# Attention and a Fourier-mixing layer on one core: which of batch 2's three token tiles is worked on alone, and first

## The chip, the cores and the metric

The kernel runs on one core of one Trainium2 chip. The core has five engines with a queue each: TensorE (PE, with its weight loads as PEld), VectorE (DVE), ScalarE (ACT), GpSimd (POOL) and SyncE (SP, which only issues DMAs here). The metric is device time in microseconds; less is better.

## The reference, cut to what matters

```python
def _attn_ref(q, k, v, tau):             # q, k, v: (8, 12, 448, 64)
    q_n = q / (norm(q, axis=-1) + 1e-06)
    k_n = k / (norm(k, axis=-1) + 1e-06)
    scores = q_n @ k_n.T / tau
    attn = softmax(scores)
    return attn @ v

def _moe_ref(x, w_ch1, w_ch2):           # x: (8, 448, 768)
    mixed = real(fft(fft(x, axis=1), axis=2))
    u = x + mixed
    un = (u - mean(u)) / sqrt(var(u) + 1e-06)     # over the last axis
    ch = relu(un @ w_ch1) @ w_ch2                 # 768 -> 3072 -> 768
    return u + ch
```

The attention's output, heads side by side, is the `x` of the second part. There are 8 batches of 448 tokens.

## The kernel before, in words

**Stages of a batch.** For each batch b the kernel loads q, k and v, normalises q and k (squares on ACT, sums on DVE, scaling on POOL, from batch 2 on with DMA transposes into `QT` and `KT`), computes scores (PE, L1464 and L1477), exponentials (ACT, L1442) and the product with v (PE, L1495 and L1501; result `X`). `ORDER` is the order of the six head pairs. Then comes the Fourier transform as matmuls with sine and cosine tables: folding of `X` on DVE (`fold`), the first product over tokens (`fs0_b`, `fs1_b`: PE, L1632 and nearby), its copy out of PSUM (`te`), the second product over features (`fd0_b`, `fd1_b`: PE, L1682 and L1685), and on DVE and ACT the sums that give `U` (`qe`, `pq`, `u`; L1713, L1716, L1727). Each row block of `U` is a token tile: its mean, variance and scale (`ba`, `bs`, `ln2`, `rs`), the normalised tile (`un`, L1779), and a DMA transpose issued by SP (`tru`, L1800) into `UNT`, where PE reads it.

**Token tiles.** A batch gives the tiles A0 (rows 0 to 127 of the first half of the transform), A1 (the mirrored rows), Yt and, shared by an even batch and the odd one behind it, Zt. `A0` and `A1` come from the transform's first half (`fd0`), Yt from its second (`fd1`); one row of A1 is copied out of Yt (`u224`, L1747), so that A1 is only whole after that copy. An even batch has three tiles in the order A0, A1, Yt, an odd one four, 28 in all.

**Pairs and singles.** The feed-forward part takes tiles in the order of batches, two at a time, except those named in `ONES`, which are taken alone:

```python
ONES = ((0, 0), (2, 2))
...
        while x < len(order):
            n = 1 if order[x] in ONES else 2
            for y in range(n):
                b, i = order[x + y]
                self.slots[b][i] = 2 * (u % 2) + y
            self.pairs.append(order[x:x + n])
            u, x = u + 1, x + n
```

`(2, 2)` is tile 2 of batch 2, Yt. `slots` says which 128 columns of `UNT` a tile's transpose fills; the units take slots 0 and 1, then 2 and 3, in turn.

A unit's work on PE is a chain in fixed order (`self.main`): the hidden layer (`h..`, from `UNT` and `W1b`, L1864: 144 matmuls, of 256 columns for a pair, of 128 for a single), whose PSUM banks ACT and DVE empty with the ReLU into `HQ` (L1880), and the second layer (L2008, 384 columns). For a pair this is a product scheme with seven block products of 12 matmuls (`m1` to `m7`) in place of eight; it needs the sums and differences `s1` to `s4` over `HQ` on DVE (L2108, six instructions) and of the weights in `TX`. For a single it is four products of 12 (`y0` to `y3`) with one sum (`s5`). The results go to `OUTB` (`fa`, `fv`, `fm`, `fin`: ACT L2029, POOL L2034, DVE L2045); `store` writes A0 with a plain DMA from SP (L2059) and the others with an indirect DMA from POOL (L2067). Between the steps of a unit PE takes attention steps of the next batch and the transform's steps.

**What sets the order.** `build` lists all steps with their dependencies and a base priority (`op.prio`), then adds to each its entry of the table `SHIFT` (some 1,870 names; the key within an entry counts the steps of that name). `Plan.schedule` then fills the queue of each engine at build time: it takes, with costs from the tables `TIMES` and `FLOW`, the step that can start first, and among those that can start at the same time the one with the lowest priority. ACT and DVE may also wait a little for a step of much lower priority number. On the chip every engine's queue is in that fixed order, with semaphore waits. `HOME` fixes the engine of some steps of the start. `Plan.fill` puts dummy matmuls (L2258) where the plan leaves PE idle for long, mostly in the first 48 us.

Of the kernel before, what the change touches and what calls it, by code (L numbers as in the profile page):

```python
# [26 lines left out]
ONES = ((0, 0), (2, 2))  # L27
# [55 lines left out]
    "iota": {0: -4743.9411}, "iotak": {0: -3749.0012}, "cst": {0: 2295.738}, "iotad": {0: 1504.4864}, "rown": {0: 3564.9514},  # L83
    "tqd": {0: 5876.6502, 1: 5614.4443}, "trd": {0: 5875.7288}, "tpd": {0: -1558.5233, 1: 550.4848}, "tad": {0: 4737.392},
    "tqs": {0: 4545.6213, 1: 5636.9779}, "trs": {0: 4448.6198}, "tps": {0: -162.6304, 1: -1607.3824}, "tas": {0: -178.9521}, "ktd0": {0: 1975.3204},
# [4 lines left out]
    "mask": {0: 35657.0228}, "sinp": {0: 48649.0823}, "half": {0: 440.6683, 1: 3500.6271}, "sinn": {0: 17464.9799}, "ldt": {0: 44319.0778},  # L90
# [883 lines left out]
class Kern:  # L974
# [857 lines left out]
    def units(self):  # L1832
# [486 lines left out]
```

## Time and profile before

| what | value |
|---|---|
| median of three runs | 575.11 us (574.59 to 575.68) |
| the profiled execution's own time | 575.0 us |
| its span, first to last instruction | 573.2 us |
| granted TensorE clock, mean | 1.000 |
| busy: PE, PEld, DVE, ACT, POOL | 553.7, 432.9, 434.0, 392.9, 224.4 us |
| HBM traffic over the span | 110 GB/s |

How to read it: times are in microseconds from the start of the span, a matmul's mean in nanoseconds. PE's matmuls are pipelined, so one that takes 326 ns by its row does not hold the next one up for as long; the pace is read from how long a run of equal matmuls takes. The chain that ended last is followed back from the last instruction, so that each of its pieces is what the next one waited for or came behind. "issue" in it, and as what ended an idle time, is time for which the profile shows no releaser. A bracket behind a row of the timeline is the idle time of the engine ahead of it.

### The profile page before, as it was taken

Reading aid. Unit: us, or ns where it says so; the run is one execution under the profiler, and the core shown is the slowest. Engines: PE = TensorE matmul, PEld = TensorE weight load, DVE = VectorE, ACT = ScalarE, POOL = GpSimd, SP = SyncE. Lnnn points to the kernel's source line nnn. Section 1 sums busy time; section 2 is a strip of 40 time slices with the busy share of each in tenths; the row PEclk is TensorE's granted clock in tenths of the full one; section 3 lists DMA queues with packets and bytes.
Section 4 is the critical chain, followed back from the end, with each engine's and each line's share of the span. In section 5 each row is a group of like instructions: output and inputs, shape, how many; then the busy total and the mean of one; then the engine's idle time right before and its main releaser. Section 6 shows DMA issues by size and latency. Waiting matters only on the chain.

```text
span 573.2 us, 16025 instructions
## 1 busy us (share of the span) xinstructions
PE 553.7 (97%) x6616; PEld 432.9 (76%) x6616; DVE 434.0 (76%) x923; ACT 392.9 (69%) x734; POOL 224.4 (39%) x332
## 2 busy tenths in 40 slices
PE   3899999999999899999999999999999999999998
PEld 2578887686787687878778688687886876959695
DVE  9889868987469867986789669965679379886353
ACT  7998976576776885578648886686665761948171
POOL 8522414356328542702380736443524003041304
PEclk9999999999999999999999999999999999999999
DMA  9999997976359645963496569461691200132001
GB/s 213 170 241 202 164 195 108 163 173 111 111 82 113 158 88 111 155 145 70 95 157 76 99 138 125 105 140 23 136 87 27 72 2 17 42 48 66 24 34 56
DMA packets 183945, 62.19 MB, mean 108 GB/s; under 512 B 166688, under 2 KB 181664, under 8 KB 183872
## 3 DMA queue, kind: packets, MB, share of 16 engines
q1 hardware_dynamic: 129824, 38.35, 35.2%
q0 software_dynamic: 54048, 22.81, 32.1%
q8 instruction: 52, 0.85, 0.6%
q14 instruction: 21, 0.17, 0.1%
HBM read 51.90 MB, written 11.01 MB: 110 GB/s over the span
## 4 chain that ended last, share of the span: by engine, by line
PE 78%; DVE 8%; ACT 6%; issue 3%; POOL 2%; DMA 2%; SPq 1%; POOLq 0%; DVEq 0%; ACTq 0%
PE PS L1864 28%; PE PS L2008 26%; PE PS L1959 7%; PE PS L1501 5%; PE PS L1464 5%; PE PS L1495 2%; PE PS L1477 1%; DMA TX<-in_q_dram 1%; ACT F L1769 1%; POOL QH L1387 1%; DVE F L1547 1%; POOL OUTB L2034 1%; PE PS L1685 1%; DVE OUTB L2045 1%; DVE X L1521 1%
## 5 line engine op out<-in xcount | busy, mean ns | idle before, releaser
L1864 PE MATMUL PS<-UNT,W1b 128*128 128x256 bf16 (+1 forms) x1728 | 185.4, 264 | 0.3 <-DVE UNT L1797 0.2
L1442 ACT ACTIVATE E<-PS 128x900 bf16<-128x900 f32 (+1 forms) x192 | 148.7, 827 | 30.3 <-PE PS L1464 24.3
L1864 PEld LDWEIGHTS PS<-UNT,W1b 128*128 128x128 bf16 x1728 | 153.4, 98 | 20.1 <-issue 1.9
L2008 PE MATMUL PS<-W2b,HQ 128*128 128x384 bf16 x720 | 124.9, 326 | 0.0
L1387 POOL TENSOR_TENSOR QH<-STG,SM 128x256 bf16<-128x256 f32 x126 | 84.4, 696 | 86.8 <-DVE SM L1177 65.0
L2008 PEld LDWEIGHTS PS<-W2b,HQ 128*128 128x128 bf16 x720 | 68.8, 98 | 43.1 <-issue 0.4
L2034 POOL TENSOR_TENSOR OUTB<-OUTB,U 128x192 f32<-128x192 f32 x72 | 51.6, 737 | 118.2 <-ACT OUTB L2029 115.6
L2008 PE MATMUL PS<-TX,HQ 128*128 128x384 bf16 (+2 forms) x444 | 76.4, 322 | 0.9 <-DVE OUTB L2045 0.5
L1880 ACT ACTIVATE HQ<-PS 128x512 bf16<-128x512 f32 x86 | 51.2, 595 | 28.8 <-PE PS L1864 27.6
L2108 DVE TENSOR_TENSOR HQ<-HQ 128x1536 bf16<-128x1536 bf16 (+1 forms) x73 | 54.1, 744 | 12.2 <-ACT HQ L1880 7.0
L2008 PEld LDWEIGHTS PS<-TX,HQ 128*128 128x128 bf16 x444 | 41.5, 98 | 27.9 <-DVE OUTB L2045 2.4
L1374 ACT ACTIVATE QH<-STG 128x384 f32<-128x384 f32 x84 | 43.1, 519 | 17.6 <-DVE SM L1376 11.6
L1376 DVE TENSOR_REDUCE SM<-QH 128x6 f32<-128x384 f32 x84 | 45.3, 544 | 11.3 <-ACT QH L1374 11.0
L1501 PE MATMUL PS<-VB,E 128*128 128x65 bf16 x1152 | 51.6, 193 | 0.0
L2067 POOL DMA_INDIRECT out_dram<-OUTB,IDX x21 | 23.7, 1127 | 69.2 <-DVE OUTB L2045 43.4
L1501 PEld LDWEIGHTS PS<-VB,E 128*128 128x128 bf16 x1152 | 47.8, 97 | 1.3
L1880 DVE TENSOR_SCALAR HQ<-PS 128x512 bf16<-128x512 f32 x40 | 27.4, 685 | 23.9 <-PE PS L1864 23.8
L1495 PE MATMUL PS<-VZ,E 128*128 128x130 bf16 x192 | 41.6, 219 | 2.0 <-issue 1.9
L1727 DVE SCALAR_TENSOR_TENSOR U<-ACG,X 128x768 bf16<-128x768 f32 (+4 forms) x39 | 39.5, 1023 | 0.9
L2029 ACT ACTIVATE OUTB<-PS 128x384 f32<-128x384 f32 x36 | 17.7, 491 | 32.2 <-PE PS L2008 29.4
L1464 PE MATMUL PS<-QK 64*128 64x225 bf16 (+2 forms) x864 | 39.2, 227 | 0.5 <-ACT QK L1290 0.5
L1464 PEld LDWEIGHTS PS<-QK 64*128 64x128 bf16 x864 | 25.6, 95 | 13.2 <-issue 6.6
(195 smaller groups left out, 784.5 us busy)
## 6 DMA issues: line engine op xcount, KB each, us to landing
STG<-in_q_dram SPq DMA_DIRECT2D x18, 384.0 KB, 3.9
STG<-in_k_dram SPq DMA_DIRECT2D x18, 384.0 KB, 3.9
VB<-in_v_dram POOLq DMA_DIRECT2D x24, 192.0 KB, 6.4
W2b<-in_moe_w_ch_dram POOLq DMA_DIRECT2D x12, 384.0 KB, 7.4
W1b<-in_moe_w_ch_dram POOLq DMA_DIRECT2D x5, 768.0 KB, 14.7
out_dram<-OUTB SPq DMA_DIRECT2D x7, 384.0 KB, 2.7
W2b<-in_k_dram SPq DMA_DIRECT2D x2, 576.0 KB, 9.1
W2b<-in_q_dram SPq DMA_DIRECT2D x2, 576.0 KB, 15.9
```

The source lines that it names most:

```text
L1374: P.add("act", lambda a, sq=sq, src=buf[:, w * x:w * x + w]: a.activation(sq, src, ACTF.Square), t_act(w), pr, f"sq{i}_{b}", reads=bn, wri ...
L1376: P.add("dve", lambda v, o=SS[:, i, H // ns * x:H // ns * (x + 1)], sq=sq: v.tensor_reduce(o, sq.rearrange("p (h d) -> p h d", d=DH), AX.X ...
L1387: r = v.tensor_tensor(v3(qh)[:, h:h + 4], v3(buf)[:, h:h + 4], RN[:, i, h:h + 4].unsqueeze(2).to_broadcast((128, 4, DH)), AluOp.mult)
L1442: return a.activation(o, self.PS[:, bk:bk + nc_, 0:SQ2], ACTF.Exp, scale=1.0 / self.tau)
L1464: i = pe.matmul(self.PS[:, bk + h, c0:c0 + n], self.KT[r, jj, kt * 128:(kt + 1) * 128], self.QT[r, jj, cols], start=True, stop=True)
L1495: r = pe.matmul(o, st(6), self.VZ[:, j, :], start=not split, stop=(split and i == 0), skip_group_check=True)
L1501: r = pe.matmul(o[:, 65 * h:65 * h + 65], st(2 * kt + h), self.VB[:, kt, 2 * j + h, :], start=(split and i == h == kt == 0), stop=((not sp ...
L1864: r = pe.matmul(self.PS[:, bk, x * n:(x + 1) * n], self.W1b[:, j, ft * 128:(ft + 1) * 128], self.UNT[:, j, cs], start=(j == 0), stop=(j == ...
L1880: return e.activation(o, i, ACTF.Relu) if e is self.nc.scalar else e.tensor_relu(o, i)
L2008: r = pe.matmul(self.PS[:, bk, 0:n], lhs(f), rhs(f), start=(start and f == 0), stop=(stop and f == NF // 2 - 1), skip_group_check=True)
L2034: r = g.tensor_tensor(self.OUTB[:, ob, xs], self.OUTB[:, ob, xs], self.U[:, ut, xs], AluOp.add)
L2108: P.add("dve", lambda v: v.tensor_tensor(cs(o), cs(a), cs(bq), op), 0.16 + 0.3 * len(ks), -0.5, f"{nm}{ks[0]}_{b}", reads=rd, writes=[x fo ...
```

## The change

The constant `ONES` names tile 0 of batch 2 in place of tile 2. So batch 2's A0 becomes a unit of its own, worked on first, and A1 and Yt form the pair behind it. A0 keeps slot 0 of `UNT`, A1 goes from slot 1 to 2, Yt from 2 to 3. Steps that carry the place of their unit in their names change them (`m10_2` becomes `m12_2`, `y02_2` becomes `y00_2`). Every entry of `SHIFT` has another number, those of the other batches and of the start too; the rest of the code, `HOME`, `TIMES` and `FLOW` among it, is the same.

```diff
-ONES = ((0, 0), (2, 2))
+ONES = ((0, 0), (2, 0))
...
 SHIFT = {
-    "iota": {0: -4743.9411}, "iotak": {0: -3749.0012}, "cst": {0: 2295.738}, "iotad": {0: 1504.4864}, "rown": {0: 3564.9514},
...
-    "un0_2": {0: 184243.4663}, "tru0_2": {0: 183025.828}, "ba1_2": {0: 182336.143}, "bs1_2": {0: 161194.5228}, "ln21_2": {0: 159526.278},
...
-    "sc_1_2": {0: 146661.6626}, "s50_2": {0: 247559.7669}, "y02_2": {0: 223949.3532, 1: 237828.8693, 2: 227136.9727},
...
+    "ln20_2": {0: 198621.6068}, "rs0_2": {0: 177910.2035}, "un0_2": {0: 167692.3748}, "tru0_2": {0: -4214.128}, "ba1_2": {0: 163988.6956},
...
+    "s50_2": {0: 238850.4958}, "y00_2": {0: 216547.338, 1: 203349.2864, 2: 206356.3583}, "y10_2": {0: 206355.5579, 1: 202008.2235, 2: 196885.558},
...
+    "s12_2": {0: 228070.3022}, "s30_2": {0: 223968.8777}, "m12_2": {0: 222836.5147, 1: 233052.5977, 2: 228875.0089}, "fa2p_2": {0: 305570.7337},
...
 }
```

More of the change, by code (lines that the diff above doesn't have):

```diff
@@ L82 @@
 SHIFT = {
-    "iota": {0: -4743.9411}, "iotak": {0: -3749.0012}, "cst": {0: 2295.738}, "iotad": {0: 1504.4864}, "rown": {0: 3564.9514},
-    "tqd": {0: 5876.6502, 1: 5614.4443}, "trd": {0: 5875.7288}, "tpd": {0: -1558.5233, 1: 550.4848}, "tad": {0: 4737.392},
-    "tqs": {0: 4545.6213, 1: 5636.9779}, "trs": {0: 4448.6198}, "tps": {0: -162.6304, 1: -1607.3824}, "tas": {0: -178.9521}, "ktd0": {0: 1975.3204},
[4 rows of a table removed]
-    "mask": {0: 35657.0228}, "sinp": {0: 48649.0823}, "half": {0: 440.6683, 1: 3500.6271}, "sinn": {0: 17464.9799}, "ldt": {0: 44319.0778},
[510 rows of a table removed]
+    "iota": {0: -14429.0048}, "iotak": {0: -8727.5871}, "cst": {0: 4382.5181}, "iotad": {0: 4872.2447}, "rown": {0: 20193.2258},
+    "tqd": {0: -6349.2577, 1: -6348.5793}, "trd": {0: 4897.335}, "tpd": {0: 18457.4759, 1: -5456.2273}, "tad": {0: 55560.9588},
+    "tqs": {0: 4920.6324, 1: 16079.43}, "trs": {0: 16715.9331}, "tps": {0: 4920.3491, 1: 1964.1555}, "tas": {0: 42801.9515}, "ktd0": {0: 5143.0165},
[4 rows of a table added]
+    "mask": {0: 36264.0626}, "sinp": {0: 49359.9216}, "half": {0: -5363.8958, 1: 34755.0483}, "sinn": {0: 63827.4273}, "ldt": {0: 76377.8819},
[507 rows of a table added]
 }
```

1020 rows, old and new, of the table SHIFT are left out of this document.

## The prediction

> **What bounds the kernel now.** I read the page's head first, then the busy time of each engine by stages, then the chain that ended last, and then the waits and the timeline of TensorE (PE) at the one place in mid-kernel where it stood still.
>
> ```profile
> span 573.2 us, 16025 instructions
> PE 553.7 (97%) x6616; PEld 432.9 (76%) x6616; DVE 434.0 (76%) x923; ACT 392.9 (69%) x734; POOL 224.4 (39%) x332
> ```
>
> The second figure of each row below is the stretch's length, the third PE's busy time in it.
>
> ```profile
> core 0: us, PE busy (x) PEld busy (x) DVE busy (x) ACT busy (x) POOL busy (x), PEclk, DMA share, GB/s
> 0.00:48.17 48.17, 35.98 (x513) 27.18 (x513) 41.85 (x106) 42.62 (x69) 23.14 (x53) 1.00 1.28 209
> 48.17:60.20 12.03, 11.10 (x174) 10.06 (x174) 11.78 (x37) 10.34 (x27) 6.25 (x8) 1.00 1.44 183
> 60.20:192.00 131.80, 131.51 (x1377) 100.06 (x1376) 103.71 (x213) 92.82 (x176) 58.69 (x78) 1.00 0.91 137
> 192.00:195.00 3.00, 1.53 (x26) 1.06 (x24) 2.94 (x8) 2.61 (x6) 1.14 (x1) 1.00 0.43 82
> 195.00:470.00 275.00, 274.86 (x3383) 217.36 (x3381) 203.76 (x431) 193.43 (x360) 108.55 (x154) 1.00 0.64 100
> 470.00:516.00 46.00, 44.08 (x491) 32.96 (x489) 42.38 (x83) 24.37 (x54) 13.34 (x15) 1.00 0.15 34
> ```
>
> From 60.2 us to 470 us PE is idle for 0.29 + 1.47 + 0.14 = 1.90 us, of which 1.47 us lie in the three microseconds around 193. Whether a busy PE is also a PE at its pace is read from the chain:
>
> ```profile
> 104.03 13.65 PE PS L2008 x84
> ...
> 195.47 3.93 PE PS L1864 x36
> ...
> 234.56 2.35 PE PS L1864 x42
> ...
> 245.32 5.20 PE PS L2008 x32
> ```
>
> The 84 products of 384 columns take 13.65 us, 162.5 ns each; the 32 of the single tile 162.5 ns each as well. A hidden layer's matmul takes 109 ns with 256 columns (3.93 us for 36) and 56 ns with 128 (2.35 us for 42). The pace is one number in places far apart, so from 60 us on the time is the count of matmuls times their pace, plus the idle time above. What is taken from that idle time comes off the end, as long as nothing later makes PE wait instead.
>
> A page of the Trainium skill speaks against this reading: "Perfetto Trace Analysis", section "Identifying the Most-Contended Engine", says that PE's busy share is no measure of how near it is to its limit, and that the weight loads' busy share is. By that, 76% here, a quarter of PE's time would be left, and later matmuls could make up a gap; I keep it as a rival. The same skill's "TensorE: Matmul & The Clock Gate", section "Back-to-back issue gap", gives columns over 2.4 plus 2.5 ns for a warm array, 162.5 ns for 384 columns, and the trace agrees to the digit.
>
> **The gap at 193 us.** PE's timeline there, with the idle time in brackets:
>
> ```profile
> 190.57 2.12 PE L2008 MATMUL PS<-TX,HQ 128*128 128x384 bf16 x12
> 192.53 0.36 PE L1477 MATMUL PS<-QK,KTD 128*128 128x225 bf16 x2
> 194.36 0.22 PE L1495 MATMUL PS<-VZ,E 128*128 128x130 bf16 x1 [1.47 <-issue]
> ...
> 195.31 4.09 PE L1864 MATMUL PS<-UNT,W1b 128*128 128x256 bf16 x36
> ```
>
> The last products of batch 1 (the first row) and a score step of batch 3 are done at 192.89. Then PE waits for a batch 3 step that needs its exponentials, and only at 195.31 come the first hidden matmuls of batch 2. These read UNT of both tiles of batch 2's pair, A0 and A1. When these were written, the normalisation (DVE) and the DMA transposes (SP's queue) show:
>
> ```profile
> 189.57 0.47 DVE L1779 TENSOR_SCALAR F<-U,MV 128x768 bf16<-128x768 bf16 x1
> ...
> 191.39 0.48 DVE L1779 TENSOR_SCALAR F<-U,MV 128x768 bf16<-128x768 bf16 x1
> ```
>
> ```profile
> 190.07 1.23 SPq L1800 DMA_TRANSPOSE UNT<-F  x1
> ```
>
> ```profile
> 191.90 1.21 SPq L1800 DMA_TRANSPOSE UNT<-F  x1
> ```
>
> ```profile
> UNT<-F SPq DMA_TRANSPOSE x24, 2.8
> ```
>
> A transpose lands 2.8 us after its issue (the median, last row). A0 is thus in place at 190.07 + 2.8 = 192.87, and A1 at 191.90 + 2.8 = 194.70. PE runs out of other work at 192.89, so the gap is the time by which A1 is late; A0 is not late. A1 must be later, because its first row is copied from tile Yt, which comes out of the second half of the transform.
>
> **The change part by part.** *The order of the tiles.* With (2, 0) alone and first, batch 2's first hidden matmul needs A0 only. It can start at about 192.9 where it started at 195.31; the attention step of 0.95 us that now stands between (194.36 to 195.31) then runs later and still has to be paid. The gain is the idle time, 1.47 us, and no more. The work moved is equal: the pair's hidden layer is 144 matmuls at 109 ns (15.7 us) with 84 products (13.65 us), the single's is 144 at 56 ns (8.1 us) with 48 products at 162.5 ns (7.8 us), 45.2 us in either order. Cost: 0.
>
> *UNT slots, transposes, SP.* A1 goes to slot 2 instead of 1 and Yt to 3 instead of 2. Those slots were last read by batch 1's second pair, whose hidden layer ends before the products of 175 us begin, and the three transposes stay three on SP's queue. A1 and Yt are needed only after the single's 15.9 us, which covers their 1.8 us and more; without that cover it would be the present 1.47 us again. Cost: 0.
>
> *Stores.* A0's store (SP) leaves sooner, A1's and Yt's scatters (POOL's queue) both at the pair's end. The counts are equal. What stands behind a scatter in POOL's queue is the scaling of the next batch's q and k. POOL is busy for 5.73 us of 17.30 in the window quoted below, which hides a scatter. Cost: 0.
>
> *DVE work that changes place.* The pair needs six sums over HQ, the single one, and these now fall into the stretch in which batch 3's transform and normalisation end. A sum over HQ is this group:
>
> ```profile
> L2108 DVE TENSOR_TENSOR HQ<-HQ 128x1536 bf16<-128x1536 bf16 (+1 forms) x73 | 54.1, 744 | 12.2 <-ACT HQ L1880 7.0
> ```
>
> Five more at 0.744 us is 3.7 us. The stretch before batch 2's first hidden matmul and that before batch 3's compare so:
>
> ```profile
> 177.50:195.50 18.00, 16.24 (x146) 10.88 (x144) 17.38 (x35) 12.82 (x29) 11.91 (x14) 1.00 1.01 126
> 236.70:254.00 17.30, 17.30 (x215) 13.83 (x213) 15.95 (x37) 11.81 (x29) 5.73 (x10) 1.00 0.90 167
> ```
>
> DVE had 17.38 of 18.00 us to do in the first, where a pair's sums lie, and 15.95 of 17.30 in the second, where the single's one lies. With 3.7 us more the second is over-full, and something must leave it for earlier. From 195 to 470 us DVE is busy 203.76 of 275 us, 74%, so there is room elsewhere. Whether the chain of batch 3 can then be early enough is read from these rows (the last attention step and the first transform step of batch 2, then of batch 3):
>
> ```profile
> 172.12 0.34 PE L1501 MATMUL PS<-VB,E 128*128 128x65 bf16 x6
> ...
> 177.52 0.56 PE L1632 MATMUL PS<-CS,F 128*97 128x225 bf16 x4
> ...
> 228.37 0.34 PE L1501 MATMUL PS<-VB,E 128*128 128x65 bf16 x6
> ...
> 236.74 0.56 PE L1632 MATMUL PS<-CS,F 128*97 128x225 bf16 x4
> ...
> 253.98 6.21 PE L1864 MATMUL PS<-UNT,W1b 128*128 128x256 bf16 x54
> ```
>
> ```profile
> 250.86 1.21 SPq L1800 DMA_TRANSPOSE UNT<-F  x1
> ```
>
> Batch 3's A1 lands now at 250.86 + 2.8 = 253.66, and its pair starts at 253.98: just in time. After the change PE comes there at 253.98 - 1.47 = 252.51. But batch 3 takes 236.74 - 228.71 = 8.0 us from its last attention step (which ends at 228.71) to its transform, and batch 2, under a fuller DVE, took 177.52 - 172.46 = 5.1 us. At batch 2's rate the transform of batch 3 begins at 233.8, and with batch 2's 194.70 - 177.52 = 17.2 us from there on, A1 lands at 251.0, 1.5 us ahead of need. I take 0, and keep 1.15 us (253.66 - 252.51) as what it costs if that chain stays where it is.
>
> *All priorities anew.* Every step's place in its queue may change, and the trace of before cannot show to what. The best that it can give beyond the gap is the remaining idle time of PE after the first hidden matmul: 0.93 + 0.29 + 0.14 + 1.92 = 3.3 us by the stage rows. The worst shown by a row is in the start, where nothing covers:
>
> ```profile
> 32.27 0.87 ACT E L1442
> ...
> 35.15 0.86 ACT E L1442
> ...
> 39.60 0.73 ACT TX L1123
> ...
> 48.17 2.87 PE PS L1864 x48
> ```
>
> The chain lies on ACT for most of the time from 31 to 44 us, and ACT is busy 42.62 of the first 48.17 us. Each piece like these put ahead of the chain is 0.7 to 0.9 us; three are 2.5 us. I take 0 between -3.3 and +2.5, since the old order leaves PE as full as the rows show and nothing in the trace says on which side of it another one falls.
>
> *Sum.* The profiled execution took 575.0 us, 573.2 of span and 1.8 around it. 575.0 - 1.47 = 573.5; the median of the three runs shown, 575.11, stands 0.1 above it, so 573.6. The gain is 0.26%, and what a measurement of this kernel can tell from no change is about 0.2%, 1.15 us: faster means below 573.96.
>
> **The rivals.** *The gap moves to batch 3 (chance 0.18).* DVE's 3.7 us stay in the over-full stretch, A1 of batch 3 lands at 253.66 as now, PE waits 1.15 us there: net gain 0.3, 574.8. For it: the two DVE shares above. Against: the 8.0 us against 5.1. A row that could push it: the same add on U takes 1.35 us while POOL scales q and k, and 0.95 us without:
>
> ```profile
> 179.96 5.58 POOL L1387 TENSOR_TENSOR QH<-STG,SM 128x256 bf16<-128x256 f32 x6 [0.17 <-DVE SM L1177]
> ```
>
> ```profile
> 183.71 1.35 DVE L1727 SCALAR_TENSOR_TENSOR U<-ACG,X 128x768 bf16<-128x768 f32 x1
> ...
> 244.22 0.95 DVE L1727 SCALAR_TENSOR_TENSOR U<-ACG,X 128x768 bf16<-128x768 f32 x1
> ```
>
> With POOL's scaling laid over batch 3's chain, two adds cost 0.8 us of the 1.5 us of room. "GPSIMD Engine Reference" of the Trainium skill, section "Specifications", lists the memory interfaces as shared, with contention for DVE instructions that have two inputs in SBUF; the two rows agree with it.
>
> *Part of the gap stays (0.11).* The first tile comes late by 0.5 to 1 us, since DVE, 97% busy there, serves other steps first. 574.2.
>
> *PE makes up gaps anyway (0.03).* Then the removal brings nothing, 575.0. The 162.5 ns are against it.
>
> *The start gets longer, and the kernel slower (0.16).* One mechanism: in ACT's queue before 44 us three pieces are put ahead of the chain to the first hidden matmul, which then comes at 50.7, not 48.17. 573.6 + 2.5 = 576.1. It decides once the start loses more than 1.47 + 1.15 = 2.6 us, about three such pieces; less makes it "no change". For it: ACT's 88% there. Against: DMA and DVE hold the chain as long, and the steps of the start are not touched by the tiles' order.
>
> *More idle time goes (0.18).* The new priorities also take some 1.4 us of the 1.92 us at 470 to 516 us or of the 0.93 us after 48 us: 572.2.
>
> **How the numbers follow.** The forecast, 573.6 us, has 0.34 and its own range of 573.0 to 574.0. Faster: 0.34 + 0.18 and a little from the edge of the partial case, 0.54. Same: the moved gap, the partial one and the made-up one, 0.30. Slower: the start, 0.16. The range reaches from 571.6 (the gap and 2 of the 3.3 us) to 576.2 (the slower case).
>
> **What would show it.** Right: no idle time of PE between batch 1's last products and the first hidden matmuls of batch 2; these have 128 columns and start within 0.3 us of A0's landing; PE's busy time changes by under 1 us outside the start. Wrong: a bracket with over 1 us of idle time at some 252 us before a 256-column group (moved gap), a first hidden matmul later than 49 us (start), or idle time over 2 us from 470 to 516.

## The result, and the profile after

The kernel after takes 581.5 us (median of four runs, 580.54 to 583.28) beside 575.35 us for the kernel before: a ratio of 1.0112 (95% interval 1.0081 to 1.0143), 1.1% slower. A second set of four runs gave 582.73 us and 1.0118 (1.0099 to 1.0136). The forecast was 573.6 us, and its range ended at 576.2. The profiled execution took 580.54 us.

The head of the page after:

```profile
span 578.7 us, 16114 instructions
PE 557.1 (96%) x6658; PEld 437.6 (76%) x6658; DVE 428.9 (74%) x917; ACT 394.0 (68%) x740; POOL 227.5 (39%) x332
```

PE is busy 3.4 us longer and issues 42 more matmuls. All 42 are dummies: their line has 204 matmuls in place of 162, of which 144 stand ahead of the first hidden matmul in both, so that behind it there were 18 and now there are 60. Line numbers are 3 lower after: the dummies stand at L2255, hidden layer and products at L1861 and L2005.

The span is 5.5 us longer. To see where, each stretch's time was taken less the pace of the matmuls in it (the prediction's 162.5, 109 and 56 ns, and for other widths a pace on the same line through these three), dummies counted as lost. What is left is the time lost on PE up to a given matmul, which can be compared where the order of the work differs. After minus before, in us:

| up to | lost, after less before | what happens in the stretch |
|---|---|---|
| batch 0's 241st hidden matmul, 81 us | -0.7 | the 18 early dummies are gone |
| batch 1's first, 118 us | +5.4 | 60 dummies, then a wait of 2.2 us |
| batch 1's 145th, 152 us | +5.9 | a wait of 0.6 us at 140 us |
| batch 2's first, 195 us | +4.9 | the gap of before shrinks |
| batch 3's 193rd, 301 us | +5.8 | new waits of 0.8 and 0.5 us at 297 and 302 us |
| batch 5's 241st, 459 us | +5.5 | no wait of over 0.4 us |
| the last matmul, 570 us | +4.5 | waits at 487 and 514 us gone, one longer |

The end of the span then lies 3.8 us behind the start of the last matmul, against 2.8. The whole loss arises between 81 and 123 us, in two pieces. The first, in the timeline of after, in the middle of the products of batch 0's single tile, (0, 0):

```profile
92.71 1.46 PE L2005 MATMUL PS<-W2b,TX 128*128 128x384 bf16 x8
94.01 3.95 PE L2255 MATMUL PS<-W1b 128*128 128x128 bf16 x60
...
97.80 1.46 PE L2005 MATMUL PS<-W2b,TX 128*128 128x384 bf16 x8
```

and of before, where the same products run through:

```profile
93.43 6.01 PE L2008 MATMUL PS<-W2b,TX 128*128 128x384 bf16 x36
```

Why are they there? `Plan.fill` puts dummies where the build-time plan has PE idle. The new priorities issue POOL's loads of the second layer's weights in another order, and the last one later:

```profile
86.18 0.71 POOL L1152 DMA_DIRECT2D W2b<-in_moe_w_ch_dram  x1 [8.95 <-DMA W2b<-in_moe_w_ch_dram]
```

```profile
79.86 0.70 POOL L1155 DMA_DIRECT2D W2b<-in_moe_w_ch_dram  x1 [2.22 <-DMA W2b<-in_moe_w_ch_dram]
```

The first row is after, the second before. The plan that the build makes (its own figures, not the chip's) has the last weights land at 95.73 us after, and at 91.66 before, and lets the third product wait for them. On the chip they landed at 90.64 us, ahead of need (before at 88.06). PE works through 60 dummies, from 94.01 us on, for weights that are already there.

The second piece is a wait for a transpose, first in the chain that ended last, then in PE's and POOL's timeline of after:

```profile
94.52 3.44 PE PS L2255 x54
97.96 4.55 PE PS L2005 x28
...
117.30 5.60 DMA UNT<-F
122.95 5.43 PE PS L1861 x48
```

```profile
116.17 1.50 POOL L2064 DMA_INDIRECT out_dram<-OUTB,IDX  x1 [12.20 <-DVE SM L1373]
...
122.95 1.27 PE L1861 MATMUL PS<-UNT,W1b 128*128 128x256 bf16 x10 [2.20 <-DMA UNT<-F]
```

The chain has the dummies in it, and then 5.6 us of one transpose, which took 2.8 us in the batches that the prediction looked at. POOL issues an indirect store (the scatter of a tile of batch 0) 1.1 us ahead of it.

The gap that the change was about, in PE's timeline of after:

```profile
196.34 2.12 PE L2005 MATMUL PS<-TX,HQ 128*128 128x384 bf16 x12 [0.23 <-DVE OUTB L2042]
198.30 0.36 PE L1474 MATMUL PS<-QK,KTD 128*128 128x225 bf16 x2
199.24 1.50 PE L1861 MATMUL PS<-UNT,W1b 128*128 128x128 bf16 x24 [0.58 <-DVE OUTB L2042]
```

Batch 2's hidden layer begins with 128 columns, 0.14 us behind A0's landing at 199.10. A0 took 3.7 us to land here, not 2.8, and the DVE step that the bracket names ends just as the matmul starts (199.24), so two waits end there almost together. Of 1.47 us idle, 0.58 are left, and 0.23 ahead of the last products. So the change did there what it says, and had lost 6 us before it came there.

### The profile page after: what moved, and what is told of

Same layout as the page of the kernel before. It is cut to its first block, busy times and chain, and to the rows that moved or that the text cites. A ratio compares the mean times of both kernels' runs of the same rounds, so it can differ in the third digit from the quotient of the medians.

```text
span 578.7 us, 16114 instructions
## 1 busy us (share of the span) xinstructions
PE 557.1 (96%) x6658; PEld 437.6 (76%) x6658; DVE 428.9 (74%) x917; ACT 394.0 (68%) x740; POOL 227.5 (39%) x332
## 4 chain that ended last, share of the span: by engine, by line
PE 80%; DVE 10%; ACT 4%; DMA 2%; POOL 2%; issue 1%; POOLq 0%; ACTq 0%; DVEq 0%
PE PS L2005 28%; PE PS L1861 27%; PE PS L1956 7%; PE PS L1498 5%; PE PS L1461 5%; ACT E L1439 2%; PE PS L1492 2%; PE PS L1474 1%; PE PS L2255 1%; DMA UNT<-F 1%; DVE SM L1250 1%; PE PS L1682 1%; PE PS L1629 1%; DMA QK<-QH 1%; DVE F L1544 1%
## 5 line engine op out<-in xcount | busy, mean ns | idle before, releaser
L1861 PE MATMUL PS<-UNT,W1b 128*128 128x256 bf16 (+1 forms) x1728 | 185.2, 264 | 3.0 <-DMA UNT<-F 2.2
L1861 PEld LDWEIGHTS PS<-UNT,W1b 128*128 128x128 bf16 x1728 | 153.8, 98 | 23.5 <-DMA UNT<-F 2.6
L2005 PE MATMUL PS<-W2b,HQ 128*128 128x384 bf16 x720 | 125.5, 326 | 0.0
L1384 POOL TENSOR_TENSOR QH<-STG,SM 128x256 bf16<-128x256 f32 x126 | 88.2, 726 | 83.1 <-DVE SM L1174 56.6
L2005 PEld LDWEIGHTS PS<-W2b,HQ 128*128 128x128 bf16 x720 | 68.7, 98 | 43.4 <-issue 0.9
L1877 ACT ACTIVATE HQ<-PS 128x512 bf16<-128x512 f32 x91 | 54.3, 597 | 43.0 <-PE PS L1861 40.6
L2005 PE MATMUL PS<-TX,HQ 128*128 128x384 bf16 (+2 forms) x444 | 76.8, 322 | 2.2 <-DVE OUTB L2042 2.2
L2005 PEld LDWEIGHTS PS<-TX,HQ 128*128 128x128 bf16 x444 | 41.6, 98 | 28.6 <-DVE OUTB L2042 3.6
L2105 DVE TENSOR_TENSOR HQ<-HQ 128x1536 bf16<-128x1536 bf16 (+1 forms) x73 | 52.8, 728 | 13.8 <-ACT HQ L1877 7.7
L2064 POOL DMA_INDIRECT out_dram<-OUTB,IDX x21 | 22.5, 1073 | 67.6 <-DVE OUTB L2042 27.0
L1877 DVE TENSOR_SCALAR HQ<-PS 128x512 bf16<-128x512 f32 x35 | 24.1, 688 | 22.6 <-PE PS L1861 22.3
L1416 POOL DMA_DIRECT2D VB<-in_v_dram x24 | 25.5, 1071 | 38.1 <-PE PS L1498 32.1
```

The source lines that it names most:

```text
L1384: r = v.tensor_tensor(v3(qh)[:, h:h + 4], v3(buf)[:, h:h + 4], RN[:, i, h:h + 4].unsqueeze(2).to_broadcast((128, 4, DH)), AluOp.mult)
L1861: r = pe.matmul(self.PS[:, bk, x * n:(x + 1) * n], self.W1b[:, j, ft * 128:(ft + 1) * 128], self.UNT[:, j, cs], start=(j == 0), stop=(j == ...
L1877: return e.activation(o, i, ACTF.Relu) if e is self.nc.scalar else e.tensor_relu(o, i)
L2005: r = pe.matmul(self.PS[:, bk, 0:n], lhs(f), rhs(f), start=(start and f == 0), stop=(stop and f == NF // 2 - 1), skip_group_check=True)
L2105: P.add("dve", lambda v: v.tensor_tensor(cs(o), cs(a), cs(bq), op), 0.16 + 0.3 * len(ks), -0.5, f"{nm}{ks[0]}_{b}", reads=rd, writes=[x fo ...
```

## The experiments

**The 60 dummies.** Left out of the kernel after:

```diff
-        self.P.fill(first, self.est - 20.0, self.id_op, warm(self.W1b[:, 0, 0:128]), 0.75)
```

> The changed kernel without the second call of fill, that is without its 60 dummy matmuls at 94 us; every other queue as in the changed kernel. Theory A (the dummies, not the data, hold PE there: the last piece of W2 had landed at 90.64 us, the dummies ran from 94.2 to 98.0): the products behind them start at 94.2, batch 1's transform and transposes come 3.5 to 3.8 us sooner, and the wait of 2.2 us for the second transpose either stays (then 581.5 - 3.6 = 577.9) or goes too (575.7). Theory B (the priorities made the data itself late, the dummies only fill a wait): PE stands idle for as long as the dummies ran, 581.5, no change. Theory C (PE waits 2.2 us for the transpose whatever comes before it, and the dummies were hidden under that chain): 579 to 581.

The run takes 575.81 us beside 575.88 for the kernel before, ratio 1.0005 (0.9993 to 1.0017): the whole loss is gone. The timeline has the products in one piece, batch 1's first hidden matmul 5.7 us earlier, and no idle time ahead of batch 2's:

```profile
92.40 5.85 PE L2005 MATMUL PS<-W2b,TX 128*128 128x384 bf16 x35
...
117.26 0.92 PE L1861 MATMUL PS<-UNT,W1b 128*128 128x256 bf16 x7 [0.50 <-issue]
...
192.24 0.36 PE L1474 MATMUL PS<-QK,KTD 128*128 128x225 bf16 x2
192.43 0.77 PE L1861 MATMUL PS<-UNT,W1b 128*128 128x128 bf16 x11
```

The reverse, 60 such dummies put into the kernel before at the same place (ten groups of six, ahead of the third product):

```diff
+        self.P.force("y001_0", 2, 10, self.id_op, warm(self.W1b[:, 0, 0:128]))
```

> The kernel before with 60 dummy matmuls put where the changed kernel has them (ahead of the product that needs the last piece of W2), nothing else changed. Theory A: they cost 60 x 58 ns = 3.5 us on PE, and the chain of batch 1 behind them shifts as much: 575.35 + 3.5 = 578.9, up to 579.2. Theory B and C (PE has 3 us of room there before batch 1's transposes): under 576.5.

578.74 us, 1.006 (1.0044 to 1.0075), which is 3.4 us by the interval's middle and 2.9 by the medians. The loss by the bookkeeping above steps up by 3.3 us at the dummies: against the kernel before it stands 0.5 us higher ahead of them, 3.8 at batch 1's first hidden matmul and 3.3 at the last matmul. The dummies in its timeline:

```profile
93.94 1.46 PE L2029 MATMUL PS<-W2b,TX 128*128 128x384 bf16 x8
...
95.24 3.51 PE L2279 MATMUL PS<-W1b 128*128 128x128 bf16 x60
...
98.59 0.65 PE L2029 MATMUL PS<-W2b,TX 128*128 128x384 bf16 x3
```

So the dummies cost some 3 of the 5.7 us; what takes the rest is the transpose's wait, which goes with them in the first run.

**What held the transpose up.** Two candidates were in the trace: the scatter ahead of it, and a block of 16,384 bytes in the instruction queue of the DMA engines at 120.95 us. The DMA view of after, 120.9 to 122.6 us, with the rate in 40 equal slices, and for each queue its packets, MB and share of 16 engines:

```profile
GB/s 151 627 259 271 265 193 18 12 72 0 0 0 0 0 0 0 0 0 0 0 0 0 6 6 6 12 6 6 12 6 12 6 12 12 6 12 6 12 12 6
q1 hardware_dynamic: 274, 0.07, 122.9%
q8 instruction: 1, 0.02, 3.4%
```

The rate counts a packet where it starts: from 121.3 us on next to none starts, while packets of q1, the queue that the transpose goes through, stay open. Queue q8 holds 52 such blocks in the whole trace, one to 256 of PE's 13,316 matmuls and weight loads. "Runtime: NRT & Kernel Launch" of the Trainium skill, section "Instruction fetch mechanics", has each engine refill its instructions in such blocks of 256, at a cost that it calls "mostly hidden"; the block's size agrees with this trace, the cost here is what the next runs measure. If the block is PE's, dummies shift it, by two instructions each (a weight load and a matmul). Theory F says that the block held the transpose up, theory S that the scatter did. Half of the dummies:

```diff
+        late = [op for op in self.P.order["pe"] if op.name == "warm" and op.start >= first]
+        self.P.order["pe"] = [op for op in self.P.order["pe"] if op not in late[1::2]]
```

> The kernel after, with every second of the ten groups of late dummies left out: 30 dummy matmuls instead of 60 ahead of the single tile's third products. The 2.2 us wait at batch 1's first hidden matmul (second transpose issued 117.30, landed 122.90) has two explanations. Theory F (instruction fetch): PE's next 16 KB of instructions were fetched at 120.95 us, in the middle of that transpose's packets, and held them up; the 60 dummies are 120 instructions that brought this fetch forward onto the transpose. With 30 dummies the fetch comes about 60 instructions later, some 3 us behind the landing, so the wait goes as well as half of the dummies: 581.5 - 1.65 - 2.2 = 577.7 us (577.2 to 578.4). Theory S (scatter): the scatter of batch 0 that POOL issues 1.1 us ahead of the transpose holds its packets up, whatever PE does; then 2.2 us stay and the time is 581.5 - 1.65 = 579.8 us (579.4 to 580.4).

578.52 us, 1.0044 (1.0027 to 1.006), between the ranges of the two theories. The transpose landed in 2.8 us and no wait followed, but the dummies did not halve:

```profile
94.87 0.50 PE L2255 MATMUL PS<-W1b 128*128 128x128 bf16 x6
...
95.84 0.84 PE L2255 MATMUL PS<-W1b 128*128 128x128 bf16 x12 [0.47 <-DVE ACG L1537]
...
96.97 0.51 PE L2255 MATMUL PS<-W1b 128*128 128x128 bf16 x6 [0.29 <-DVE F L1544]
...
97.78 0.51 PE L2255 MATMUL PS<-W1b 128*128 128x128 bf16 x6 [0.30 <-DVE SM L1373]
98.12 1.14 PE L2005 MATMUL PS<-W2b,TX 128*128 128x384 bf16 x6
```

`fill` gives each group a dependency on the DVE step that the plan has ahead of it. The 30 hold PE from 94.87 to 98.12, 3.25 us, waiting for steps of DVE; the 60 took 3.8. With 0.55 us saved in place of 1.65, theory F's sum, made again after the run, is 581.5 - 0.55 - 2.2 = 578.8. The error was in my price of a dummy. And 42 more:

```diff
+        for op in late[:7]:
+            new = Op(("pe",), op.fn, (0.34,), 0, "warm")
+            new.eng, new.start, new.end, new.deps = "pe", op.start, op.end, set(op.deps)
+            self.P.order["pe"].insert(self.P.order["pe"].index(op) + 1, new)
```

> The kernel after, with seven of the ten groups of late dummies doubled: 102 dummy matmuls instead of 60. The 42 more cost 42 x 0.055 = 2.3 us of PE. Theory F (instruction fetch): 84 instructions more move PE's fetch ahead of the second transpose of batch 1, so the wait of 2.2 us goes: 581.5 + 2.3 - 2.2 = 581.6 us (580.9 to 582.4), more dummies at no cost, and that transpose lands within 3 to 4 us of its issue. Theory S (scatter): the wait stays, 583.8 us (583.3 to 584.5).

580.73 us, 1.0077 (1.0063 to 1.009), just below theory F's range: more dummies, and less time than with 60. The block came at 115.45 us, 5.6 us ahead of the transpose, which landed in 2.8. In these two runs, however, POOL had also issued the scatter 0.6 us earlier against the transposes, so they do not part the candidates. The next one does: 24 dummies less at the start, and nothing changed near the wait.

```diff
+        self.P.order["pe"] = [op for op in self.P.order["pe"] if not (op.name == "warm" and 39.0 < op.start < 40.4)]
```

> The kernel after, with its 60 dummies at 94 us, the scatter and all queues as they are, and without 24 of the dummies at the start (40.3 to 41.8 us, where PE has nothing else to do until its next operand is there). This takes 48 instructions out of PE's stream 55 us ahead of the disputed wait and changes nothing near it, but PE's fetch comes 48 instructions later there. Theory F (instruction fetch): the fetch now comes behind the landing of batch 1's second transpose, that transpose lands some 2.8 us after its issue, and the 2.2 us go: 582.1 - 2.2 = 579.9 us (579.2 to 580.7), 1.007 times the kernel before. Any cause in the scatter or in the order of the queues: the wait stays, 582.1 us (581.4 to 583.0), 1.011 times the kernel before. A start that gets longer by over 0.5 us without these dummies would show at the first hidden matmul (48.5 to 48.7 us in the kernel after).

The ratio is the one expected of theory F, 1.0074 (1.0054 to 1.0095); the median, 580.97 us, lies between the two ranges, in a set where the kernel before took 576.32. In the profile the first hidden matmul came 1.1 us later than in that of after, but PE was 1.1 us later at 36 us already, ahead of the place of the edit. Counted from batch 0's 241st hidden matmul to batch 1's first, the loss grows by 4.0 us, against 5.8 in both profiles of after. So 1.8 us went, but not all of the wait:

```profile
117.91 1.50 POOL L2064 DMA_INDIRECT out_dram<-OUTB,IDX  x1 [12.34 <-DVE SM L1373]
...
122.86 1.38 PE L1861 MATMUL PS<-UNT,W1b 128*128 128x256 bf16 x11 [0.44 <-DMA UNT<-F]
```

The DMA rates over the 5.65 us from the issue of batch 1's second transpose, in 40 slices, first of after, then of this run, go alike up to 3.4 us (slice 24) and part there; the block of after starts at 3.65 us:

```profile
GB/s 0 0 0 0 0 0 304 391 304 391 522 261 565 44 40 151 214 248 228 221 164 95 147 199 111 250 265 74 13 0 0 0 5 9 9 9 9 13 254 266
```

```profile
GB/s 0 0 0 0 0 0 304 391 304 391 522 261 565 44 38 143 207 250 239 223 160 123 158 214 212 216 207 210 158 27 0 0 13 38 116 178 201 199 208 254
```

Side by side, in us against the issue of batch 1's second transpose (idle time by the matmuls' pitch, so 0.1 to 0.2 above the brackets):

| kernel | scatter issued | block of instructions at | landed | PE idle |
|---|---|---|---|---|
| after | -1.1 | +3.7 | +5.6 | 2.4 |
| after, second profile | -1.1 | +3.7 | +5.7 | 2.3 |
| 24 fewer dummies at 40 us | -1.1 | +7.1 | +3.8 | 0.6 |
| no late dummies | -1.1 | +10.5 | +3.9 | 0.7 |
| 30 dummies | -1.8 | +7.3 | +2.8 | 0 |
| 102 dummies | -1.8 | -5.6 | +2.8 | 0 |

Both theories were half right: the meeting with the block of instructions costs PE some 1.7 us; the other 0.6 stay with the scatter right ahead, and the last run below tests them. The block comes later with 48, 60 and 120 instructions fewer in PE's queue, and earlier with 84 more, so it is PE's. Why POOL came 0.6 us later with the scatter in four of the six is open. The repeat of the kernel after was meant to show whether single runs escape the meeting:

> The kernel after, unchanged, with more runs and another profile. Theory F says that the 2.2 us are a meeting of PE's instruction fetch with the second transpose of batch 1. In the run of the old order with the new priorities the same 60 dummies stood in the same place, the fetch came 0.5 us later against the transpose, and no wait followed. So single runs should fall into two groups, about 579.3 us without the meeting and 581.5 us with it, with a median from 579.5 to 581.5 us. If the profile shows the fetch inside the transpose's packets, batch 1's first hidden matmul comes at 122.9 us; if not, by 121.5 us. Theory S (scatter) and any cause in the order of the queues: every run has the wait, and the profile shows it again whatever the fetch does.

They do not: 580.72 to 583.13 us, with a median above the expected range, no group near 579, and the profile has the block at the same +3.7 us. My expectation of two groups rested on the run of one half (below), whose scatter was early too.

**The halves of the change.** The priorities of after with batch 2's tile in its old place (`ONES = ((0, 0), (2, 2))` in after), one run:

> One half of the change alone: the priorities of the kernel after, with batch 2's single tile behind its pair as in the kernel before. If the early loss of the kernel after comes from the priorities and not from the order of the tiles, the 60 dummies stand again at 94 us and batch 1's first hidden matmul comes at 122.9 us (122.0 to 123.5), 5 us later than the 117.55 of the kernel before. If the order makes it, it comes by 118.5 us. From batch 2 on these priorities fit the other order, and the whole time is expected well above both kernels, 590 to 605 us.

603.18 us. Batch 1's first hidden matmul came at 121.49 us, outside the expected range but 3.9 us later than before, behind the same 60 dummies:

```profile
118.24 3.12 SPq L1797 DMA_TRANSPOSE UNT<-F  x2
121.49 0.71 PE L1861 MATMUL PS<-UNT,W1b 128*128 128x256 bf16 x5
```

The transposes were not held up here: the scatter went 1.7 us ahead, and the second one had landed by the time the block came (+4.1 us). So the dummies belong to the priorities and not to the order of the tiles. Ahead of batch 2 the loss grows by 1.2 us in this run, as in the kernel before: the priorities alone do not close the gap. The new order with the priorities of before, one run:

> The other half of the change alone: batch 2's single tile ahead of its pair, with the priorities of the kernel before. Up to batch 1's first hidden matmul nothing differs from the kernel before: no dummies near 94 us, that matmul at 117.5 us (117.0 to 119.0). If the order alone takes away the wait ahead of batch 2, PE is idle there for 0.7 us or less in one piece, against 1.5 us in the kernel before; the rival is that it takes the new priorities too, and the wait stays at 1.2 us or more. From there on these priorities fit the other order, so that the whole time is expected well above both kernels, 585 to 600 us.

592.92 us; batch 1's first hidden matmul at 117.80, no dummies near 94 us, and at batch 2:

```profile
192.78 0.36 PE L1477 MATMUL PS<-QK,KTD 128*128 128x225 bf16 x2
193.33 0.89 PE L1864 MATMUL PS<-UNT,W1b 128*128 128x128 bf16 x13 [0.20 <-DMA UNT<-F]
```

The order alone closes the gap. The rest of both times comes of priorities that go with the other order: behind the first hidden matmul there are 438 dummies in the run of 603.18 us and 258 in this one, most of them ahead of batch 3's hidden layer. How much of the time is theirs and how much PE would have waited without them was not parted.

**Where the gap's 1.5 us went.** Without the dummies, the time should be 1.5 us below the kernel before, and it is not. First a control, the kernel before without its own 18 late dummies (the same line left out):

> The kernel before, without its 18 late dummy matmuls (51 to 55 us by its plan, in front of batch 0's hidden matmuls). Control for the run of the kernel after without its 60. If dummies cost their own time wherever real work is ready, 18 x 0.055 = 1.0 us goes at 50 to 63 us; what stays of it at the end is between 0.3 us (what the kernel after without late dummies kept at batch 1's first hidden matmul) and 1.3 us (what it kept at 69 us): 575.9 - 0.8 = 575.1 us (574.5 to 575.6 beside 575.9 for the kernel before). Rival: the dummies do what they are there for and hold the granted clock; without them the mean clock falls below 0.995 and the time is at least 576.9 us.

575.85 us beside 575.9, ratio 1.0 (0.9991 to 1.001). The 0.8 us that I expected did not come, and nothing was lost; leaving the dummies out is not what hides the gain. The loss from 152 us on, by the same bookkeeping, says more. The table has its growth since batch 1's 145th hidden matmul, in us, in the three profiles of the kernel before and its variants, and in seven of after and its variants (without the next run):

| up to | before: mean (range) | after: mean (range) | after less before |
|---|---|---|---|
| batch 2's first | +1.2 (+1.2 to +1.3) | -0.3 (-0.5 to +0.3) | -1.5 |
| batch 3's first | -0.3 (-0.7 to +0.3) | -1.9 (-2.4 to -0.8) | -1.5 |
| batch 3's 193rd | -1.7 (-2.2 to -1.1) | -2.1 (-2.7 to -1.1) | -0.4 |
| the last matmul | -5.1 (-5.5 to -4.8) | -6.0 (-6.7 to -4.7) | -0.9 |

The gap's 1.5 us are still there at batch 3's first hidden matmul, and 1.1 of them go between that and the 193rd: there the loss falls by 1.3 to 1.4 us in each of the three, and by 0.3 at the most in each of the seven. From the start of the last matmul to the end of the span it takes 3.7 us in the mean, against 3.1 (2.8 to 3.3 before, 3.1 to 3.9 after), for a cause that was not tried. So some 0.3 us of the 1.5 reach the end, less than the interval tells from nothing. Two waits take the 1.1 us, shown in the run without late dummies:

```profile
291.28 2.12 PE L2005 MATMUL PS<-TX,HQ 128*128 128x384 bf16 x12 [0.64 <-DVE OUTB L2042]
...
296.38 1.00 PE L1625 MATMUL PS<-CS,F 128*128 128x113 bf16 x16 [0.35 <-DVE F L1589]
```

Both are waits for DVE. Two of its drains were moved:

```diff
+        for op, to, step in ((at["fin11_3"][0], at["ss6_5"][0], 0), (at["fin10_3"][0], at["e1_4"][0], 1)):
+            dve.remove(op)
+            dve.insert(dve.index(to) + step, op)
```

> The kernel after without its 60 late dummies, and with two drains of batch 3's products moved in DVE's queue: the one that PE waits for at 290.31 us (0.8 us of idle time) ahead of the sum of squares that stands before it, and another, at 293.68 us, behind the two additions that the next transform waits for (0.5 us of idle time of PE at 295.75). These two waits are where the run without dummies gave back most of the 1.5 us that it had gained ahead of batch 2. If they are the price, 0.5 to 0.9 us come back: 575.8 - 0.7 = 575.1 us (574.7 to 575.5), 0.8 below the kernel before. Rival: DVE is full there, and the next wait takes the gain, as it did when the 18 dummies of the kernel before were left out: 575.7 us or more, no difference from before.

576.77 us beside 576.18, 1.001 (0.9995 to 1.0025): the gain that I expected did not come. The first wait fell to 0.18 us and the second went, and the moved drain then came too late for the bank that it empties:

```profile
292.27 2.12 PE L2005 MATMUL PS<-TX,HQ 128*128 128x384 bf16 x12 [0.18 <-DVE OUTB L2042]
...
297.54 1.49 PE L1861 MATMUL PS<-UNT,W1b 128*128 128x256 bf16 x12 [1.83 <-DVE OUTB L2042]
```

The rival was right: one wait was traded for another, a larger one. Last, the rest at batch 1, from the run without late dummies:

```diff
+        op = [x for x in pool if x.name == "sc_1_0"][0]
+        pool.remove(op)
+        pool.insert(pool.index([x for x in pool if x.name == "sc3_2"][0]) + 1, op)
```

> The kernel after without its 60 late dummies, and with batch 0's scatter of the second tile moved in POOL's queue from ahead of batch 1's second transpose to behind the first scaling of q and k that follows it. In the kernels without the meeting of fetch and transpose (no late dummies; 24 fewer dummies at the start) that transpose still lands 3.8 us after its issue, with the scatter's packets right ahead of its own, and PE waits 0.6 to 0.7 us for it. If the scatter is the cause of this rest, the transpose lands within 2.9 us and PE waits at most 0.1 us ahead of batch 1's first hidden matmul; the whole time is then 575.8 - 0.6 = 575.2 us where no later wait takes it (574.7 to 575.7, beside 576.0 for the kernel before). If the wait stays at 0.5 us or more, the rest has another cause. Rival for the time alone: the wait goes and a later one takes its place, no difference from before.

574.7 us beside 575.96, ratio 0.9975 (0.996 to 0.9989). The transpose lands 2.8 us after its issue, and neither of the two early hidden layers waits:

```profile
117.82 1.36 PE L1861 MATMUL PS<-UNT,W1b 128*128 128x256 bf16 x11
118.26 1.10 POOL L2064 DMA_INDIRECT out_dram<-OUTB,IDX  x1 [0.29 <-POOL QH L1384]
...
192.67 0.36 PE L1474 MATMUL PS<-QK,KTD 128*128 128x225 bf16 x2
192.88 1.33 PE L1861 MATMUL PS<-UNT,W1b 128*128 128x128 bf16 x21
```

This version beats both, by 1.4 us against the kernel before (1.3 by the medians). That this is about what the gap was worth is not shown to be more than chance, as most of that had been given back at batch 3. Against the run without late dummies it is 1.1 us by the medians, of which the wait taken away explains 0.6; the rest is open, since the execution that was profiled, 574.93 us, is no faster than that of the kernel before (575.0).

## Why the prediction was wrong

- *PE's pace decides, and a gap comes off the end.* Right. With the dummies put into the kernel before, PE stood 3.8 us behind after them and still 3.3 us at the last matmul: it made up next to nothing. The formula that the prediction quotes is given in the Trainium skill's "TensorE: Matmul & The Clock Gate", section "Back-to-back issue gap", for a single isolated matmul, with other spacings for a stream of them; here the streams kept its 162.5 and 56 ns.
- *The gap at 193 us, -1.47.* Right in place and size: 1.5 to 1.7 us in seven of the eight profiles of after and its variants, 1.0 in the first of after. The single's matmuls start 0.14 us behind A0's landing, in after (199.10) and in the run of the new order alone (193.19). The order alone does it.
- *The gap moves to batch 3.* It did not: the 1.5 us are still there at batch 3's first hidden matmul. To that point the zero taken for the DVE sums that move was right; whether they have a part in the waits for DVE behind it was not tried.
- *"As long as nothing later makes PE wait instead".* The sum had no term for it. At 290 to 303 us new waits for DVE took some 1.1 of the 1.5 us, and the end of the span is 0.6 us longer. So even without the dummies the forecast of 573.6 us would have been some 2 us too low: the run without them took 575.81.
- *All priorities anew, 0 between -3.3 and +2.5.* This is the step that failed. It cost 6.1 us between 81 and 123 us: 3.3 to 3.8 for dummies, 2.4 for the transpose. That the work stays equal, "Cost: 0", held for the layers only, and the zero for the stores did not reckon with a scatter that comes right ahead of a transpose (0.6 us of the 2.4). The upper bound came from the start, as the place "where nothing covers", by rows of ACT. But priorities also set POOL's order, and so when weights are due in the plan; and the dummies follow from the plan. The dummies' line was in the text ahead of the prediction, and "mostly in the first 48 us" was read as if they could not come elsewhere. The trace of before had a pointer: 18 of its dummies ran from 54.1 to 57.5 us, within batch 0's hidden layer.
- *The slower rival (the start).* Right in sign, wrong in place: the first hidden matmul came at 48.66 us against 48.17, short of the 49 us that the prediction names, and within the 48.1 to 50.3 of the other profiles.
- *What would show it.* "PE's busy time changes by under 1 us outside the start" was the sign that told: it grew by 3.4 in all, and the dummies at 94 us alone are 3.95.

## What to carry to other kernels

A table of priorities changes more than the order of the work: whatever the build derives from its plan (dummies, load order) is changed with it, so a change of priorities is priced by everything that the planner emits, and the count of instructions of each engine is the first thing to compare. Filler work that waits for a planned time is not free: it stands in the queue ahead of real work that is ready, and costs the time until its own last dependency. In this kernel a transpose that PE needs at once came 1.0 us sooner with no indirect store right ahead of it.

## What the runs showed of the hardware that was not expected

In this kernel a 16 KB block of instructions fetched while a DMA transpose was under way held it up. At batch 1 the transpose landed 5.6 us after its issue with the block, and 3.8 without it, behind the same scatter. Over the thirteen profiles, of the 246 transposes into `UNT` whose landing the trace tells, the 36 with such a block starting 1.0 to 2.7 us after their issue landed after 4.4 us in the median, the other 210 after 2.8. That is a correlation, with exceptions: 6 of the 36 landed within 3 us, and 28 of the 210 took over 4. An indirect store issued 1.1 us ahead of a transpose added 1.0 us to it (3.8 against 2.8). So instructions added to PE can make a DMA late that has nothing to do with them, and taking 24 dummies out at 40 us brought some 1.7 us at 122 us.
